# Fused attention and two feed-forward layers: low parts of the second layer's weights made by adding transfers, 16 weights converted early

## The chip, the cores and the metric

The kernel runs on one core of a Trainium2 chip. The metric is the device time of one launch in microseconds (us), the median of several runs; lower is better.

## What is computed

The reference chains three blocks, all in float32. The weights arrive as 64-bit floats.

```python
scores = scale * np.matmul(q, k.transpose(0, 1, 3, 2))        # 2 x 12 heads, 448 x 448, head 64
scores = np.einsum('bhij,hg->bgij', scores, w_pre)            # heads mixed before the softmax
attn = softmax(scores)
attn = np.einsum('bhij,hg->bgij', attn, w_post)               # and after it
x = np.matmul(attn, v)                                        # 896 tokens x 768
h = x @ w_in;  x = (h * sigmoid(1.702 * h)) @ w_out           # first layer, 768 -> 2048 -> 768
h = x @ w_in2; out = (P(h) / Q(h)) @ w_out2                   # second layer, cubic over quadratic
```

## The kernel before, in words

**Stages.** The attention takes some 240 us, the first layer follows to about 476 us, the second to the end. The attention works in chunks of 120 query rows and groups of 10 rows by 12 heads: scores (line 301), a transfer that regroups rows (330), a matmul that mixes heads (335), maximum, exponential, normalising, the second mix (368), and the product with v (387).

**The layers.** A layer has 32 *up* steps (16 column tiles `ft`, two halves of the tokens each, 18 matmuls of 448 columns) and 24 *down* weights (four groups `qq` of six, 24 matmuls for both halves). Each operand is kept as a high part, rounded to the matmul's format, and a low part, the rest; three matmuls (high by high, low weight by high, high by low) give one product (lines 613 to 615 and 680 to 682). So every weight tile needs, before TensorE may use it, a high part `w[:, 0]` and a low part `w[:, 1]`. `up` weights are 128x768, `down` weights 128x512; there are three buffers `wu` for the first and three `wd` for the second.

**Converting a weight.** `w_load` (564) brings the 64-bit words into a `raw` buffer on GpSimd's queue, two or three transfers for each weight. ScalarE takes the magnitude (`w_mag`, 569), VectorE makes the 32-bit float out of the words in four steps (`w_bits`, 574, 576, 578, 581) in a `wm` buffer. For the first layer the high part is then a cast (`w_part` with rest false, line 598 through 229 on ScalarE or 231 on VectorE) and the low part a subtraction on VectorE (595 through 234). The second layer's 40 weights (16 up, 24 down) are converted ahead, during the attention and the first layer, and stored as 32-bit floats in DRAM (`w_store`, 587, tiles d1u and d1d); in the second layer `w_fetch` (591) brings them back into a `raw` buffer, from which high and low parts are made in the same way. There are two raw buffers during the attention and three afterwards; a raw buffer is free again when the low part is made.

**The order of work.** A planner (`Plan.issue`) plays all steps through with estimated costs, each step having a rank, and writes each engine's instructions in the order in which its play issues them. It is a fixed order on each engine and queue: an instruction that waits holds back all behind it. Where the play finds TensorE busy for less than 55% of the last 2.6 us and nothing to do, it puts in pairs of matmuls on a tile of ones (`filler`, line 223), whose result nobody reads. `EARLY` is the number of second-layer weights whose ranks are spread over the attention; the others have ranks in the first layer, though a step can be issued before its rank's time where its engine has nothing else ready.

**The passage from attention to first layer.** The buffers of the attention are given up and those of the layers are set up when the last product with v is done (`open_late`, 512): a small transfer brings in `cab` (528), ScalarE takes absolute values of two of its columns (529), and everything behind that on ScalarE waits for it.

Of the kernel before, what the change touches and what calls it, by code (L numbers as in the profile page):

```python
# [12 lines left out]
AF = mybir.ActivationFunctionType  # L13
ALU = mybir.AluOpType
# [16 lines left out]
W_LAG = 4500  # L31

RANK = dict(k=-45, q=-45, v=-45, sc=-14, sco=-14, rg=-37, pre=-3, max=-3, exp=-6, n0=-9, n1=-9, n2=-4, post=1, phi=-4)
# [8 lines left out]
    whi=dict(act=0, dve=800),  # L42
    wlo=dict(dve=0),
# [12 lines left out]
NQ = NF // FQ  # L56
TB = 12
TAIL = 2
EARLY = 24
MID = 54  # L60
QC = 1.0 + 1e-6

# [128 lines left out]
def f(ap):  # L191
    return ap.bitcast(F32)
# [10 lines left out]
def talking_heads_then_two_ffn(ctx: ExitStack, tc: tile.TileContext, q, k, v, wpre, wpost, win1, wout1, win2, wout2, ab, out):  # L203
    nc = tc.nc
    pe, act, dve, pool, sp = nc.tensor, nc.scalar, nc.vector, nc.gpsimd, nc.sync
# [21 lines left out]
    def cast(eng, o, i):  # L227
        if eng is act:
            act.activation(o, i, AF.Copy)  # L229
        else:  # L230
            dve.tensor_copy(o, i)

    def sub(eng, o, a, b):
        eng.tensor_tensor(o, a, b, ALU.subtract)  # L234
# [30 lines left out]
    t_ = {}  # L265
# [157 lines left out]
    def step(name, ways, ns, deps, rank, fn, *args, **kw):  # L423
        if isinstance(ways, str):
            ways = [(ways, ns)]
        ways = [(*w, 0)[:3] for w in ways]
        plan.add(name, ways, deps, rank, lambda e: fn(*[engines[e] if x is None else x for x in args]), **kw)


    def copying(n, who, psum=False):  # L430
        cost = {"act": 94 - 42 * psum + 0.833 * n, "dve": 60 + (1.05 if psum else 0.54) * n}
        return [(e, cost[e], x) for e, x in PREF[who].items() if x is not None]

    def joining(n, who):
        cost = {"dve": 68 + 1.042 * n, "pool": 149 + 2.103 * n}
        return [(e, cost[e], x) for e, x in PREF[who].items() if x is not None]
# [3 lines left out]
    def mark(name, deps, give):  # L440
        plan.add(name, (), deps, 0, give=give)
# [11 lines left out]
    for ci, (b, c) in enumerate(chunks):  # L453
# [5 lines left out]
        for hp in range(NP):  # L459
            if ci == 0 and hp in (2, 3):  # L460
                for o in range(2):
                    n, e = (("sc1", 0, hp), ("sco1", 0, hp)) if o else (("sc", 0, hp), ("sco", 0, hp))
# [70 lines left out]
    def held(b, *n):  # L533
        k = plan.bank[n, b]
        if b == "wu" and not tiles[b]:
            wu = keep.tile([128, H * S], F32R, tag="wu", name="wu")
            tiles[b] = [wu[:, 2 * DM * i : 2 * DM * (i + 1)] for i in range(3)]
        if k >= len(tiles.get(b, ())):
            open_late()
        return tiles[b][k]  # L540
# [7 lines left out]
    def wcols(key):  # L548
        return DM if key[1] == "u" else FQ * 128
# [41 lines left out]
        pool.dma_start(t_["wf", key], t_["wd", key])  # L591

    def w_part(key, eng, rest):
        if rest:
            sub(eng, t_["w", key][:, 1], f(t_["wf", key]), f(t_["w", key][:, 0]))
        else:
            w = t_["w", key] = held("w" + key[1], "whi", key)[:, : 2 * wcols(key)].rearrange("p (s f) -> p s f", s=2)
            cast(eng, w[:, 0], f(t_["wf", key]))

    XN = {}  # L600

# [128 lines left out]
    for u in units:  # L730
        key = (u[1], "u", u[2]) if u[0] == "up" else (u[1], "d", u[2] * KK + u[3])
# [4 lines left out]
    def w_steps(key, c, rk):  # L736
        step(("wmag", key), "act", 90 + 760 * c, [d_raw[key]], rk + RANK["wmag"], w_mag, key, take=["wm"])
        for i in range(4):
            d0 = [("wb", key, i - 1)] if i else [("wmag", key)]
            kw = dict(give=[("raw", d_raw[key])]) if i == 3 else {}  # L740
            step(("wb", key, i), "dve", 60 + (400, 400, 810, 810)[i] * c, d0, rk, w_bits, key, i, **kw)
# [3 lines left out]
    for key, us in uses.items():  # L745

        p = NG - 30 + 8 * key[2] if key[:2] == (0, "u") and key[2] < 3 else rank[us[0]]
        c = wcols(key) / DM
        if key in ahead:
            j = ahead.index(key)  # L750
            e = (NG - 12) * (j + 0.5) / EARLY + RANK["ahead"]
            if j >= EARLY:
                e = NG + RANK["ffn"] + MID * (j - EARLY + 0.5) / (len(ahead) - EARLY)
            step(("eld", key), "pool", 3600 * c, [("hold",)], e + RANK["wld"], w_load, ("eld", key), key, take=["raw"], lag=W_LAG)
            w_steps(key, c, e + RANK["wb"])
            step(("est", key), "pool", 2000 * c, [("wb", key, 3)], e, w_store, key, give=[("wm", ("wmag", key))], lag=W_LAG)
            step(("wld", key), "pool", 2000 * c, [("est", key)], p + RANK["wld"], w_fetch, key, take=["raw"], lag=W_LAG)
            src = ("raw", ("wld", key))
        else:
            step(("wld", key), "pool", 3600 * c, [("hold",)], p + RANK["wld"], w_load, ("wld", key), key, take=["raw"], lag=W_LAG)  # L760
            w_steps(key, c, p + RANK["wb"])
            src = ("wm", ("wmag", key))
        d0 = [("wld", key) if key in ahead else ("wb", key, 3)]
        step(("whi", key), copying(wcols(key), "whi"), 0, d0, p + RANK["whi"], w_part, key, None, False, take=["w" + key[1]])
        step(("w", key), joining(wcols(key), "wlo"), 0, [("whi", key)], p + RANK["wlo"], w_part, key, None, True, give=[src])
        mark(("wend", key), us, [("w" + key[1], ("whi", key))])
    chunks_of = [[ci for ci, (b, c) in enumerate(chunks) if b == hf] for hf in range(2)]
    for L in range(2):
        for ft in range(NF):
            qq = ft // FQ  # L770
            for hf in range(2):
                key = (L, ft, hf)
                u = ("up",) + key
                p = rank[u]
# [37 lines left out]
        for qq in range(NQ):  # L812
            for u in downs(L, qq):
                _, _, _, m, halves = u
                p = rank[u]
# [88 lines left out]
```

## Time and profile before

| | before |
|---|---|
| time, median of 3 runs | 713.13 us (712.88 to 713.31) |
| span of the profiled execution, first to last instruction | 712.1 us |
| the profiled execution's own time | not listed; the runs' median is 1.0 us above its span |
| TensorE busy | 704.0 us (99%), 4230 matmuls |
| VectorE busy | 557.3 us (78%) |
| ScalarE busy | 406.7 us (57%) |
| GpSimd busy | 162.7 us (23%) |
| granted clock of TensorE | 0.999 |

The matmuls are pipelined: the busy time of one reaches into the next. What a matmul costs in a stream is the distance from its start to the next one's start; in the layers these distances are 0.2 us, where a single matmul's row says 0.37. So a busy share of 99% says that TensorE had something to do, and lost time must be looked for in the distances.

### The profile page before, as it was taken

How to read it: one execution, taken by the hardware profiler on the slowest of the kernel's cores; microseconds unless marked ns; L12 is line 12 of the kernel's file. 1: busy time of each engine (PE TensorE's matmuls, PEld its weight loads, DVE VectorE, ACT ScalarE, POOL GpSimd, SP SyncE). 2: the span in 40 equal slices, each digit the busy share in tenths (PEclk: the TensorE clock that was granted, in tenths of full speed). 3: DMA queues.
4: the chain of work that ended last, by engine and by line, in shares of the span. 5: the costliest groups of instructions: out<-in, count | busy, mean ns of one | idle time of the engine just before them, and what ended most of it. 6: DMA issues, size and time to landing. Idle time of an engine off the chain costs nothing.

```text
span 712.1 us, 11642 instructions
## 1 busy us (share of the span) xinstructions
PE 704.0 (99%) x4230; PEld 599.7 (84%) x4230; DVE 557.3 (78%) x1109; ACT 406.7 (57%) x764; POOL 162.7 (23%) x300
## 2 busy tenths in 40 slices
PE   8999999999999999999999999999999999999997
PEld 5666767767768889999999999999999999999997
DVE  2778678787888488887988898969999699789632
ACT  3678686786786445555452443348887565357310
POOL 0423222321323343343333323110001100100000
PEclk9999999999999999999999999999999999999999
DMA  5888877686563555555554544331112212111122
GB/s 190 247 264 278 285 234 250 221 280 220 177 222 129 175 172 185 183 187 176 178 177 163 161 143 168 112 100 52 53 38 60 81 38 74 53 30 29 31 82 104
DMA packets 40215, 106.85 MB, mean 150 GB/s; under 512 B 6622, under 2 KB 20446, under 8 KB 40158
## 3 DMA queue, kind: packets, MB, share of 16 engines
q0 software_dynamic: 23040, 76.89, 33.2%
q1 hardware_dynamic: 16830, 28.85, 11.9%
q8 instruction: 33, 0.54, 0.3%
q10 hardware_dynamic: 288, 0.37, 0.1%
q14 instruction: 24, 0.20, 0.1%
HBM read 71.49 MB, written 15.34 MB: 122 GB/s over the span
## 4 chain that ended last, share of the span: by engine, by line
PE 94%; DMA 3%; DVE 1%; ACT 1%; issue 1%; POOL 0%; ACTq 0%; DVEq 0%; SPq 0%
PE mm L680 11%; PE mm L682 11%; PE mm L681 11%; PE bk L613 11%; PE bk L614 11%; PE bk L615 10%; PE bk L368 10%; PE bk L335 9%; PE bk L387 5%; PE mm L301 5%; DMA d1u<-wmk 1%; DMA raw<-in_wout_dram 1%; PE bk L223 1%; DMA T<-S 0%; DMA cab<-in_ab_dram 0%
## 5 line engine op out<-in xcount | busy, mean ns | idle before, releaser
L680 PE MATMUL mm<-g,wd 128*128 128x448 f32 x384 | 141.7, 369 | 0.0
L682 PE MATMUL mm<-g,wd 128*128 128x448 f32 x384 | 140.3, 365 | 0.0
L681 PE MATMUL mm<-g,wd 128*128 128x448 f32 x384 | 140.2, 365 | 0.0
L368 PEld LDWEIGHTS bk<-W,E 120*112 120x112 f32 (+1 forms) x720 | 84.2, 177 | 33.6 <-issue 22.2
L368 PE MATMUL bk<-W,E 120*112 120x120 f32 (+1 forms) x720 | 88.2, 268 | 0.0
L335 PE MATMUL bk<-T,wpr 120*120 120x448 f32 (+1 forms) x180 | 81.8, 547 | 0.7 <-DMA T<-S 0.7
L680 PEld LDWEIGHTS mm<-g,wd 128*128 128x128 f32 x384 | 72.1, 188 | 5.8
L682 PEld LDWEIGHTS mm<-g,wd 128*128 128x128 f32 x384 | 72.1, 188 | 5.7
L681 PEld LDWEIGHTS mm<-g,wd 128*128 128x128 f32 x384 | 72.2, 188 | 5.4
L564 POOL DMA_DIRECT2D rawk<-in_win_dram x81 | 44.9, 561 | 136.5 <-issue 18.1
L341 DVE TENSOR_REDUCE sm<-bk 120x1 f32<-120x448 f32 (+1 forms) x90 | 55.7, 620 | 25.3 <-PE bk L335 24.3
L613 PE MATMUL bk<-xh,wu 128*128 128x448 f32 x192 | 70.7, 368 | 1.5 <-ACT t L623 1.5
L614 PE MATMUL bk<-xh,wu 128*128 128x448 f32 x192 | 70.3, 366 | 0.5 <-DVE wu L234 0.5
L613 PE MATMUL bk<-xn,wu 128*128 128x448 f32 x192 | 70.4, 367 | 0.0
L615 PE MATMUL bk<-xh,wu 128*128 128x448 f32 x192 | 70.2, 366 | 0.0
L614 PE MATMUL bk<-xn,wu 128*128 128x448 f32 x192 | 70.1, 365 | 0.0
L615 PE MATMUL bk<-xn,wu 128*128 128x448 f32 x192 | 70.1, 365 | 0.0
L237 DVE TENSOR_TENSOR yt<-mm,yt 128x896 f32<-128x896 f32 (+1 forms) x43 | 40.2, 936 | 36.9 <-PE mm L682 36.0
L229 ACT ACTIVATE AT<-bk 112x480 f32<-112x480 f32 (+1 forms) x87 | 50.4, 580 | 27.2 <-PE bk L368 26.5
L564 POOL DMA_DIRECT2D rawk<-in_wout_dram x70 | 38.7, 558 | 96.4 <-issue 26.1
L347 ACT ACTIVATE E<-bk,sm 120x448 f32<-120x448 f32 (+1 forms) x90 | 56.5, 628 | 3.5 <-DVE sm L341 1.6
L634 DVE SCALAR_TENSOR_TENSOR t<-t,cab,bk 128x448 f32<-128x448 f32 x64 | 43.4, 678 | 15.9 <-ACT t L630 10.9
(109 smaller groups left out, 1301.1 us busy)
## 6 DMA issues: line engine op xcount, KB each, us to landing
rawk<-in_win_dram POOLq DMA_DIRECT2D x81, 256.0 KB, 3.9
T<-S SPq DMA_DIRECT2D x86, 210.0 KB
rawk<-in_wout_dram POOLq DMA_DIRECT2D x70, 256.0 KB, 3.5
raw<-in_wout_dram POOLq DMA_DIRECT2D x26, 256.0 KB, 3.2
d1d<-wmk POOLq DMA_DIRECT2D x22, 256.0 KB, 4.4
d1u<-wmk POOLq DMA_DIRECT2D x28, 192.0 KB, 4.6
rawk<-d1u POOLq DMA_DIRECT2D x14, 384.0 KB, 3.3
raw<-in_win_dram POOLq DMA_DIRECT2D x15, 256.0 KB, 3.1
```

Of the source, the lines that this page charges most:

```text
L229: act.activation(o, i, AF.Copy)
L335: pe.matmul(p[:K, :S], wpr[:K, :K], t_["T", t][:K], start=True, stop=True)
L341: dve.tensor_reduce(t_["sm", t][:K, 0:1], t_["pre", t][:K, :S], AX.X, ALU.max, negate=True)
L347: act.activation(t_["E", t][:K], t_["pre", t][:K, :S], AF.Exp, bias=sm[:K, 0:1], scale=1.0, accum_out=sm[:K, 1:2])
L368: pe.matmul(o, t_["E", t][:K, jc * CP : jc * CP + CP], t_["W", t][:K], start=True, stop=True)
L564: pool.dma_start(r[:, c : c + 256], src[:, c : c + 256])
L613: pe.matmul(p[:, :S], w[:, 0, ws], x[:, 0, kk], start=kk == 0, stop=False)
L614: pe.matmul(p[:, :S], w[:, 1, ws], x[:, 0, kk], start=False, stop=False)
L615: pe.matmul(p[:, :S], w[:, 0, ws], x[:, 1, kk], start=False, stop=kk == KK - 1)
L680: pe.matmul(p[:, hf, :S], w[:, 0, ms], gt[:, 0, i, cs], start=i == 0, stop=False)
L681: pe.matmul(p[:, hf, :S], w[:, 1, ms], gt[:, 0, i, cs], start=False, stop=False)
L682: pe.matmul(p[:, hf, :S], w[:, 0, ms], gt[:, 1, i, cs], start=False, stop=i == FQ - 1)
```

## The change

Four things are changed. The low part of a second-layer weight is no longer a subtraction on VectorE: ScalarE writes the negative of the high part into the place of the low part (`w_minus`, a new step `wn`), and a transfer on GpSimd's queue adds the 32-bit weight from the raw buffer to it (`accum_op=ALU.add`). `EARLY` goes from 24 to 16. The planner's costs for the queue's steps are lowered (3600 to 2000, 2000 to 1200 and 2000 to 700 ns). With these the planner writes a new order on all engines.

```diff
-EARLY = 24
+EARLY = 16
...
     def w_part(key, eng, rest):
-        if rest:
+        if rest and eng is pool:
+            pool.dma_start(t_["w", key][:, 1], f(t_["wf", key]), accum_op=ALU.add)
+        elif rest:
             sub(eng, t_["w", key][:, 1], f(t_["wf", key]), f(t_["w", key][:, 0]))
...
+    def w_minus(key):
+        act.activation(t_["w", key][:, 1], f(t_["w", key][:, 0]), AF.Copy, scale=-1.0)
...
-            step(("eld", key), "pool", 3600 * c, [("hold",)], e + RANK["wld"], w_load, ("eld", key), key, take=["raw"], lag=W_LAG)
+            step(("eld", key), "pool", 2000 * c, [("hold",)], e + RANK["wld"], w_load, ("eld", key), key, take=["raw"], lag=W_LAG)
...
-            step(("est", key), "pool", 2000 * c, [("wb", key, 3)], e, w_store, key, give=[("wm", ("wmag", key))], lag=W_LAG)
-            step(("wld", key), "pool", 2000 * c, [("est", key)], p + RANK["wld"], w_fetch, key, take=["raw"], lag=W_LAG)
+            step(("est", key), "pool", 1200 * c, [("wb", key, 3)], e, w_store, key, give=[("wm", ("wmag", key))], lag=W_LAG)
+            step(("wld", key), "pool", 700 * c, [("est", key)], p + RANK["wld"], w_fetch, key, take=["raw"], lag=W_LAG)
...
-        step(("w", key), joining(wcols(key), "wlo"), 0, [("whi", key)], p + RANK["wlo"], w_part, key, None, True, give=[src])
+        if key[0] == 0:
+            step(("w", key), joining(wcols(key), "wlo"), 0, [("whi", key)], p + RANK["wlo"], w_part, key, None, True, give=[src])
+        else:
+            step(("wn", key), "act", 52 + 0.833 * wcols(key), [("whi", key)], p + RANK["wlo"], w_minus, key)
+            step(("w", key), "pool", 700, [("wn", key)], p + RANK["wlo"], w_part, key, None, True, give=[src], lag=5000)
```

Line numbers of the changed kernel are larger: by 5 from `up` on (618 stands for 613, 628 for 623), the adding transfer is line 595 and the negative copy line 603.

**ScalarE at the passage from the attention to the first layer.** `xh` is the last chunk's attention output, `t` the gate's result (line 623, then 628), `wu` a weight's high part. Before:

```order
L229 ACTIVATE xh_1700<-bk_67 128x3x88
L529 ACTIVATE cab<-cab 128x2
L623 ACT_TABLE_LOAD
L623 ACTIVATE t_2495<-bk_69 128x448
L229 ACTIVATE xh_1700<-bk_68 128x3x88
L229 ACTIVATE g_2493<-t_2495 128x448
L623 ACTIVATE t_2496<-bk_66 128x448
L569 ACTIVATE wmk_81<-rawk_79 128x768
```

and now:

```order
L229 ACTIVATE xh_1686<-bk_69 128x3x88
L529 ACTIVATE cab<-cab 128x2
L569 ACTIVATE wm_2453<-rawk_78 128x768
L229 ACTIVATE xh_1686<-bk_66 128x3x88
L628 ACT_TABLE_LOAD
L628 ACTIVATE t_2459<-bk_67 128x448
L229 ACTIVATE g_2457<-t_2459 128x448
L569 ACTIVATE wmk_80<-rawk_79 128x512
L229 ACTIVATE wu<-wmk_81 128x768
```

The first gate result frees bank 69 before and bank 67 now, and the second half of `xh` has moved ahead of it; the cast of the fourth weight, `wu<-wmk_81`, stands two rows behind that gate's high part.

**VectorE, the conversion of the fourth up weight** (the first `wu` that is not made during the attention). Before, the steps 574 to 581 on `wmk_80` and the low part stand among the first layer's work on `g`:

```order
L574 TENSOR_SCALAR wmk_80<-wmk_80 128x768
L576 TENSOR_SCALAR wmk_80<-wmk_80 128x768
L578 SCALAR_TENSOR_TENSOR wmk_80<-rawk_78,wmk_80 128x768
L234 TENSOR_TENSOR g_2493<-t_2496,g_2493 128x448
L581 SCALAR_TENSOR_TENSOR wmk_80<-rawk_78,wmk_80 128x768
L231 CAST g_2493<-t_2497 128x448
L234 TENSOR_TENSOR wu<-wmk_80,wu 128x768
```

and now its last two steps, on `wmk_81`, stand among the maxima of the attention's last groups:

```order
L341 TENSOR_REDUCE sm_2286<-bk_67 120x1
L578 SCALAR_TENSOR_TENSOR wmk_81<-rawk_78,wmk_81 128x768
L341 TENSOR_REDUCE sm_2296<-bk_69 120x1
L353 TENSOR_SCALAR sm_2286<-sm_2286 120x1
L581 SCALAR_TENSOR_TENSOR wmk_81<-rawk_78,wmk_81 128x768
L355 RECIPROCAL sm_2286<-sm_2286 120x1
```

The conversion moved from behind the fourth gate result into the attention.

**GpSimd's queue where the second layer's fetches begin.** Before, fetches alone:

```order
L587 DMA d1d_4148<-wmk_81 128x512
L591 DMA rawk_78<-d1u_517 128x768
L591 DMA rawk_79<-d1u_565 128x768
L591 DMA rawk_78<-d1u_682 128x768
L591 DMA raw_2488<-d1u_727 128x768
```

and now fetches and adding transfers (595) in turn:

```order
L591 DMA raw_2452<-d1u_514 128x768
L591 DMA rawk_78<-d1u_538 128x768
L595 DMA wu<-raw_2452 128x768
L591 DMA rawk_79<-d1u_669 128x768
L591 DMA raw_2452<-d1u_700 128x768
L595 DMA wu<-rawk_78 128x768
L595 DMA wu<-rawk_79 128x768
L591 DMA rawk_78<-d1u_853 128x768
L591 DMA rawk_79<-d1d_860 128x512
L595 DMA wd_2454<-rawk_79 128x512
L591 DMA rawk_79<-d1u_996 128x768
```

A fetch into a raw buffer now stands behind the adding transfer that reads that buffer, on the same queue.

## Rows read from the trace of the kernel before

**Rows 1.** The page: shares of the chain that ended last.
```profile
PE 94%; DMA 3%; DVE 1%; ACT 1%; issue 1%; POOL 0%; ACTq 0%; DVEq 0%; SPq 0%
```
**Rows 2.** Waits of TensorE: us in total, times, longest.
```profile
PE bk L613 <- ACT t L623: 1.5, 1, 1.5
```
**Rows 3.** TensorE in order of time: start us, us, instruction, idle before and releaser.
```profile
240.79 0.37 PE L615 MATMUL bk<-xh,wu 128*128 128x448 f32 x1
242.68 0.47 PE L613 MATMUL bk<-xh,wu 128*128 128x448 f32 x1 [1.51 <-ACT t L623]
242.98 0.36 PE L614 MATMUL bk<-xh,wu 128*128 128x448 f32 x1
243.18 0.36 PE L615 MATMUL bk<-xh,wu 128*128 128x448 f32 x1
...
257.37 1.73 PE L223 MATMUL bk<-warm 128*128 128x240 f32 x14
258.93 0.43 PE L613 MATMUL bk<-xh,wu 128*128 128x448 f32 x1
259.89 0.47 PE L614 MATMUL bk<-xh,wu 128*128 128x448 f32 x1 [0.52 <-DVE wu L234]
...
325.95 0.61 PE L223 MATMUL bk<-warm 128*128 128x240 f32 x4
326.40 0.36 PE L613 MATMUL bk<-xh,wu 128*128 128x448 f32 x1
```
**Rows 4.** ScalarE in order of time, at the passage and before the fourth weight's cast.
```profile
240.58 0.20 ACT L529 ACTIVATE cab<-cab 128x2 f32<-128x2 f32 x1 [3.43 <-DMA cab<-in_ab_dram]
240.79 1.28 ACT L623 ACT_TABLE_LOAD   x1
242.08 0.54 ACT L623 ACTIVATE t<-bk 128x448 f32<-128x448 f32 x1
242.52 0.39 ACT L229 ACTIVATE xh<-bk 128x264 fp32r<-128x264 f32 x1
...
258.01 0.84 ACT L229 ACTIVATE wu<-wmk 128x768 fp32r<-128x768 f32 x1
258.74 0.90 ACT L569 ACTIVATE wmk<-rawk 128x768 f32<-128x768 f32 x1
```
**Rows 5.** VectorE in order of time, the fourth up weight.
```profile
255.65 0.95 DVE L581 SCALAR_TENSOR_TENSOR wmk<-rawk,wmk 128x768 int32<-128x768 int32 x1
...
258.88 0.96 DVE L234 TENSOR_TENSOR wu<-wmk,wu 128x768 fp32r<-128x768 f32 x1 [0.34 <-ACT wu L229]
```
**Rows 6.** The chain that ended last, pieces in time: start us, us, what.
```profile
39.31 1.00 PE bk L368 x8
...
41.07 0.82 PE bk L368 x8
```
**Rows 7.** Groups of VectorE: low parts of fetched weights; busy us, mean ns.
```profile
L234 DVE TENSOR_TENSOR wu<-rawk,wu 128x768 fp32r<-128x768 f32 x14 | 13.4, 954 | 0.3
...
L234 DVE TENSOR_TENSOR wd<-rawk,wd 128x512 fp32r<-128x512 f32 x14 | 9.6, 683 | 0.0
```
**Rows 8.** Stretches: us, busy us of PE, PEld, DVE, ACT, POOL; clock, DMA share, GB/s.
```profile
245.00:455.00 210.00, 209.48 (x1044) 193.86 (x1043) 181.04 (x294) 95.66 (x152) 74.53 (x135) 1.00 0.51 170
476.00:703.00 227.00, 227.00 (x1125) 210.16 (x1124) 178.25 (x290) 130.03 (x221) 18.29 (x34) 1.00 0.18 55
481.00:534.00 53.00, 53.00 (x263) 48.83 (x262) 51.53 (x88) 43.53 (x79) 4.30 (x8) 1.00 0.16 48
```
**Rows 9.** Issues on GpSimd's queue: KB each, median us from issue to landing.
```profile
rawk<-d1u POOLq DMA_DIRECT2D x14, 384.0 KB, 3.3
...
rawk<-d1d POOLq DMA_DIRECT2D x14, 256.0 KB, 3.0
```
**Rows 10.** The last down weight: ScalarE's cast, and the unit that TensorE starts then.
```profile
693.31 0.19 PE L673 MATMUL mm<-warm 128*128 128x64 f32 x1
...
693.51 0.63 ACT L229 ACTIVATE wd<-rawk 128x512 fp32r<-128x512 f32 x1 [4.24 <-PE mm L682]
```

More of the change, by code (lines that the diff above doesn't have):

```diff
@@ L753, in talking_heads_then_two_ffn @@
                 e = NG + RANK["ffn"] + MID * (j - EARLY + 0.5) / (len(ahead) - EARLY)
-            step(("eld", key), "pool", 3600 * c, [("hold",)], e + RANK["wld"], w_load, ("eld", key), key, take=["raw"], lag=W_LAG)
+            step(("eld", key), "pool", 2000 * c, [("hold",)], e + RANK["wld"], w_load, ("eld", key), key, take=["raw"], lag=W_LAG)
             w_steps(key, c, e + RANK["wb"])
-            step(("est", key), "pool", 2000 * c, [("wb", key, 3)], e, w_store, key, give=[("wm", ("wmag", key))], lag=W_LAG)
-            step(("wld", key), "pool", 2000 * c, [("est", key)], p + RANK["wld"], w_fetch, key, take=["raw"], lag=W_LAG)
+            step(("est", key), "pool", 1200 * c, [("wb", key, 3)], e, w_store, key, give=[("wm", ("wmag", key))], lag=W_LAG)
+            step(("wld", key), "pool", 700 * c, [("est", key)], p + RANK["wld"], w_fetch, key, take=["raw"], lag=W_LAG)
             src = ("raw", ("wld", key))
         else:
-            step(("wld", key), "pool", 3600 * c, [("hold",)], p + RANK["wld"], w_load, ("wld", key), key, take=["raw"], lag=W_LAG)
+            step(("wld", key), "pool", 2000 * c, [("hold",)], p + RANK["wld"], w_load, ("wld", key), key, take=["raw"], lag=W_LAG)
             w_steps(key, c, p + RANK["wb"])
```

## The prediction

> **What bounds the kernel now.** I read first the chain that ended last: 94% of it is TensorE [rows 1]. So time can be won or lost only where TensorE does something needless or stands still. The list of its waits is short, and the longest is 1.5 us [rows 2]. Because a busy matmul row hides small gaps, I then read TensorE in order of time and took the distances from start to start. In a stream of 448-column matmuls it is 0.20 us (242.98 to 243.18), and an up step of 18 starts 3.65 us after the one before, a down unit of 24 some 4.87 us. After the start-up I find three places where the distance is larger or the work is idle, all in the first layer [rows 3]:
>
> - At 240.79 the next matmul starts 1.89 us later, 1.69 more than the stream.
> - At 257.37 stand 14 matmuls on the tile of ones, 1.56 us; then one real matmul, after which 0.96 us pass, 0.76 too many.
> - At 325.95 stand 4 more of them, 0.45 us.
>
> Together 4.46 us. Everything else, the whole second layer included, runs at the pace of the matmuls: TensorE is busy for 227.00 of 227 us there [rows 8]. That sets the size of what can be expected: the gain cannot be much over 4.5 us, whatever VectorE is relieved of, while a new wait can cost any amount.
>
> **What causes the three places.** The first is the passage out of the attention. ScalarE waits 3.43 us for the transfer of `cab`, then loads a table for 1.28 us, and only then makes the first gate result, which frees the bank that TensorE wants [rows 4]. The second is the fourth up weight: its last conversion step runs at 255.65, its high part at 258.01 behind a gate, its low part at 258.88 [rows 4, 5]; the planner saw this coming and put the 14 idle matmuls there. The third place is planned alike.
>
> **The change part by part.** *Subtractions removed.* 16 of 0.954 us and 24 of 0.683 us [rows 7] are 31.7 us of VectorE in the second layer. VectorE is busy for 178 of 227 us there, TensorE waits for it nowhere [rows 8]: worth nothing to the time.
>
> *Negative copies added.* 40 on ScalarE. No row shows this copy; the high part's cast has the same shape and engine, 0.84 us for an up weight [rows 4] and 0.63 for a down weight [rows 10], so about 28.6 us. ScalarE goes from 130 to some 159 of 227 us. The tight piece is 481 to 534, where it is busy for 43.5 of 53 us [rows 8]: some 9 weights pass there (40 x 53/227), 7 us more, about 50.5 of 53. VectorE, at 51.5 now, falls to about 44 in the same piece, and each gate passes through both engines, so I cost the exchange at nothing. Its cover is the rest of ScalarE's idle time there, 2.5 us; without it up to 3 us.
>
> *Adding transfers.* 40 more on GpSimd's queue, 0.54 us of issue each (18.29 us by 34 [rows 8]). What is unknown is L, the time from issue to landing; no row of before shows such a transfer. The nearest is the fetch of the same bytes on the same queue: 3.3 us for an up weight, 3.0 for a down weight [rows 9]. The Trainium skill speaks against taking that: "Collectives: The Full Stack", section "The bandwidth ceiling: the fold count and why AG ≠ RS ≠ AR", says that an add inside the DMA engines needs two source reads instead of one and so ran at half a copy's rate; no run here shows it yet, and by it 3.3 us would become at most 6.6, still inside the room worked out next. My own bounds are the fetch's 3.0 and twice 3.3, since the transfer has a sum to form and its destination to read; I take 5, the middle.
>
> The room: a down weight's buffer is free when its unit ends, and two more units run before the weight is wanted, 9.74 us. The chain is now 0.20 us hand-over (693.31 to 693.51), cast 0.63, 0.20, copy 0.63, 0.20, issue 0.54, then L [rows 10]: 2.4 + L, so L may be 7.3. For an up weight the two units are four up steps, 14.6 us, and the chain 2.8 + L: 11.8. The queue has its own limit. A fetch must wait until the transfer that reads its raw buffer has landed, and behind a waiting fetch stand the next weights' transfers. The new order has 25 turns from a transfer to a fetch; if each cost L, with 80 issues of 0.54, the queue needs 25 L + 43 us, and 227 us are there: L may be 7.35. At 5 both have room: 168 us of queue, and 2.3 us at the tightest weight. Raw buffers stay held some 6 us longer, but (11.6 us a cycle over three) gives one weight in 3.9 us where one in 5.7 is used. Cost: nothing.
>
> *The new order.* This is where I expect the gain. At the passage TensorE now has 60 matmuls (12.2 us) between the last product with v and the first bank that needs a gate result, against 12 (2.4 us) before. It would ask for that bank 9.8 us after 240.99, at 250.8, and the gate, now behind a magnitude (0.90) and the `xh` cast (0.39), ends at 242.62 + 1.29 = 243.9 [rows 4]. The 1.69 us go. The second half of `xh` is late next: cast by 242.1, VectorE about 0.4 after it, wanted after 30 matmuls, at 244.7. The fourth up weight's conversion has moved into the attention, and its cast stands two rows behind the first gate's high part, so it is ready by about 250 where before it was 259.8. The 0.76 us go, and there is no need for the 14 idle matmuls; the order holds neither these nor the 4: 1.56 and 0.45 us go.
>
> *What pays for it.* By the order, the attention converts 25 weights in place of 27 and the first layer 55 in place of 53. Two weights are at most eight steps of 0.96 us, 7.7, less three subtractions of 0.95 and one of 0.68 that leave this stage: VectorE gets about 4 us more where it has 29 idle (210 - 181 [rows 8]). Nothing. In the attention, the mix behind a scores block costs 1.00 us instead of 0.82 [rows 6], and the new order has 13 such places instead of 11: 0.4 us more.
>
> Sum: -1.69 - 1.56 - 0.76 - 0.45 + 0.4 = -4.1 us. The span becomes 708.0; the runs' median lies 1.0 us above the span of the profile, so **709.1 us**.
>
> **The rivals.** *A slow landing* (the other side). If L is over 7.3, every turn of the queue and every down weight at the end waits. At L = 7.6 the queue needs 233 us where 227 are there, 6 too many, and the last down weights come 0.3 us late, two or three times: 709.1 + 7 = 716. Each further 0.1 us of L adds up to 2.5. For it speaks only that the operation is unseen; against it that fetches land in 3.3, and that the queue does nothing else there.
>
> *The idle matmuls only stood in for a wait.* If the fourth weight is as late as now, or another takes its place, TensorE stands still in their stead. Gone is then at most the 1.69 of the passage, less the 0.4: about 711.8, perhaps 712.5. Against it speaks the place of the conversion in the new order.
>
> *ScalarE becomes late* between 481 and 534: up to 3 us come back, 709 to 712. For it speaks 95% load on an engine that works in a fixed order behind VectorE's results; against it that TensorE works through banks ahead of the gates, and that VectorE is faster there.
>
> **How the numbers follow.** The measurement can tell about 0.2% from no change, 1.4 us. The forecast, 708.2 to 710.5, gets 0.62, all faster. ScalarE late gets 0.14 (0.10 faster, 0.04 the same), idle matmuls that stood for a wait 0.12 (the same), the slow landing 0.12 (slower). Faster 0.72, the same 0.16, slower 0.12. The range goes from 708.2, where even the 0.4 of the attention fails to appear and other small gaps close, to 713.2, above the second and third rival; it leaves out the slow landing and a little at both ends.
>
> **What would show it.** Right: no distance over 0.3 us near the passage and at the fourth up weight, 28 of the filler matmuls of 240 columns instead of 46, no wait of TensorE for `wu` or `wd`, adding transfers landing in 3 to 6.6 us, VectorE's busy time lower by some 28 us. Wrong: TensorE waiting for a DMA into `wu` or `wd` in the second layer; fetches on GpSimd's queue that wait longer than 7 us for a transfer; a gap of TensorE in the first layer that ends with a weight's low part.

## The result, and the profile after

The changed kernel takes 722.85 us by the median (720.86 to 724.34), the kernel before 713.02 in the same session: a ratio of 1.0134, with an interval of 1.0116 to 1.0152. It is slower by 1.3%; 709.1 us was predicted, with a range up to 713.2. The profiled execution's span is 720.7 us against 712.1, 8.6 more.

What TensorE waits for now, in us in total, times, and the longest; no wait of this kind over 0.2 us stood there before:

```profile
PE bk L335 <- ACT AT L229: 7.2, 4, 3.8
PE bk L368 <- ACT AT L229: 2.1, 1, 2.1
```

Both belong to the attention: `AT` holds the attention weights that ScalarE copies out of a PSUM bank behind the second mix, and L335 and L368 want that bank. The stretches, first of the kernel before, then of the changed one (columns as in [rows 8]). The last three are taken 8.6 us later than in [rows 8], since the layers start that much later now, so that they hold the same pieces of work:

```profile
20.00:240.00 220.00, 219.76 (x1844) 158.66 (x1841) 169.71 (x477) 159.68 (x357) 64.18 (x117) 1.00 0.70 231
```

```profile
20.00:240.00 220.00, 210.55 (x1690) 147.62 (x1687) 161.03 (x452) 153.56 (x349) 56.79 (x104) 0.99 0.65 217
253.60:463.60 210.00, 210.00 (x1039) 194.15 (x1038) 189.73 (x316) 102.51 (x161) 83.18 (x150) 1.00 0.56 185
484.60:711.60 227.00, 227.00 (x1126) 210.41 (x1125) 152.79 (x249) 155.06 (x262) 50.55 (x69) 1.00 0.46 104
489.60:542.60 53.00, 53.00 (x264) 49.13 (x263) 48.61 (x85) 49.35 (x89) 12.54 (x17) 1.00 0.44 93
```

TensorE lost 9.2 us in the attention, where it had been busy throughout. The first layer has no idle stretch any more (210.00 against 209.48, and none of the 18 idle matmuls), and the second is as full as before, with VectorE lighter by 25 us and ScalarE heavier by 25. So TensorE went through the layers as predicted, and the loss lies ahead of them: the 8.6 us, and the 4.46 that the layers gained and the total does not show, 13.1 us.

**Where one stall comes from.** The largest stands between 90.58 and 95.33. The chain of waits there (start us, us, what):

```profile
84.21 0.21 POOL d1u L587
84.42 0.32 issue
84.74 9.07 DMA d1u<-wmk
...
93.92 0.07 ACT wmk L569
...
94.71 0.58 ACT AT L229
95.29 0.04 issue
95.33 1.05 PE bk L335 x2
```

A weight's store reads `wmk` for 9.07 us. ScalarE wants to write the next magnitude (L569) into that buffer, and behind it in ScalarE's fixed order stands the copy `AT`. ScalarE and then TensorE in order of time (start us, us, instruction, idle before and releaser):

```profile
89.43 0.20 ACT L347 ACTIVATION_READ_ACCUMULATOR E<-bk,sm 120x1 f32 x1
93.92 0.89 ACT L569 ACTIVATE wmk<-rawk 128x768 f32<-128x768 f32 x1 [4.28 <-DMA d1u<-wmk]
94.71 0.57 ACT L229 ACTIVATE AT<-bk 112x480 f32<-112x480 f32 x1
```

```profile
20.88 1.76 PE L335 MATMUL bk<-T,wpr 120*120 120x448 f32 x4
...
90.58 0.98 PE L368 MATMUL bk<-W,E 120*112 120x120 f32 x8
95.33 1.05 PE L335 MATMUL bk<-T,wpr 120*120 120x448 f32 x2 [3.77 <-ACT AT L229]
...
97.78 2.57 PE L335 MATMUL bk<-T,wpr 120*120 120x448 f32 x4
```

TensorE stands still for 3.77 us, and then four matmuls take 2.57 us that take 1.76 elsewhere. The stretches ahead of and behind this stall (the third number from the end is the granted clock, as a share of full speed):

```profile
84.00:90.00 6.00, 6.00 (x53) 4.67 (x50) 3.26 (x10) 2.85 (x7) 2.89 (x6) 1.00 1.02 318
...
95.30:100.30 5.00, 4.97 (x16) 3.04 (x16) 3.40 (x12) 3.47 (x10) 0.00 (x0) 0.66 0.28 99
```

At 0.66 instead of 1.00 for 5 us, the stall costs an estimated 1.7 us more (5 times 0.34).

The other four stalls of TensorE are of the same kind. ScalarE's magnitudes ahead of them, each with `AT` as the next instruction behind it:

```profile
56.91 0.89 ACT L569 ACTIVATE wmk<-rawk 128x768 f32<-128x768 f32 x1 [1.83 <-DMA d1u<-wmk]
...
61.69 0.89 ACT L569 ACTIVATE wmk<-rawk 128x768 f32<-128x768 f32 x1 [1.73 <-DMA d1u<-wmk]
...
124.77 0.90 ACT L569 ACTIVATE wmk<-rawk 128x768 f32<-128x768 f32 x1 [1.52 <-DMA d1u<-wmk]
...
130.49 0.89 ACT L569 ACTIVATE wmk<-rawk 128x768 f32<-128x768 f32 x1 [2.68 <-DMA d1d<-wmk]
```

Behind them TensorE waits 1.32, 1.43, 0.69 and 2.06 us; with the 3.77 these are all its waits for `AT`.

ScalarE's waits for such stores, over the whole run:

```profile
ACT wmk L569 <- DMA d1u<-wmk: 9.8, 5, 4.3
...
ACT wmk L569 <- DMA d1d<-wmk: 5.0, 3, 2.7
```

Before, they were 1.2 and 1.0 us. By the median the stores of the attention have not become slower: from issue to landing they took 5.1 us before (3.1 to 8.9) and take 4.8 now (3.2 to 9.6). At this place they are 1 to 2 us slower. What shrank more is the room. GpSimd's issues and ScalarE's magnitudes in the kernel before, at the like place:

```profile
80.09 1.08 POOL L587 DMA_DIRECT2D d1u<-wmk  x2
...
82.54 0.55 POOL L587 DMA_DIRECT2D d1d<-wmk  x1
```

```profile
87.96 0.92 ACT L569 ACTIVATE wmk<-rawk 128x768 f32<-128x768 f32 x1
91.11 0.67 ACT L569 ACTIVATE wmk<-rawk 128x512 f32<-128x512 f32 x1
```

There, 7.9 and 8.6 us lie between a store's issue and the magnitude, which finds its buffer free. In the changed kernel ScalarE comes to the magnitude at 89.6, 5.4 us after the issue at 84.20. The planner works out that room: it counts an up weight's store as done 1200 + 4500 ns after its issue now, 2000 + 4500 before. Here the store took 9.07 us.

### The profile page after: what moved, and what is told of

Same layout as the page of the kernel before. It is cut to its first block, busy times and chain, and to the rows that moved or that the text cites. A ratio compares the mean times of both kernels' runs of the same rounds, so it can differ in the third digit from the quotient of the medians.

```text
span 720.7 us, 11680 instructions
## 1 busy us (share of the span) xinstructions
PE 705.4 (98%) x4212; PEld 599.0 (83%) x4212; DVE 529.5 (73%) x1063; ACT 435.3 (60%) x810; POOL 198.8 (28%) x340
## 4 chain that ended last, share of the span: by engine, by line
PE 92%; DMA 5%; ACT 1%; issue 1%; DVE 0%; POOL 0%; SPq 0%; ACTq 0%
PE mm L685 11%; PE bk L618 11%; PE bk L620 11%; PE bk L619 11%; PE mm L687 11%; PE mm L686 11%; PE bk L368 9%; PE bk L335 8%; PE mm L301 5%; PE bk L387 4%; DMA d1u<-wmk 2%; DMA T<-S 2%; DMA d1d<-wmk 1%; PE bk L223 0%; ACT AT L229 0%
## 5 line engine op out<-in xcount | busy, mean ns | idle before, releaser
L368 PEld LDWEIGHTS bk<-W,E 120*112 120x112 f32 (+1 forms) x720 | 84.3, 178 | 37.1 <-issue 19.6
L368 PE MATMUL bk<-W,E 120*112 120x120 f32 (+1 forms) x720 | 89.6, 270 | 2.2 <-ACT AT L229 2.1
L335 PE MATMUL bk<-T,wpr 120*120 120x448 f32 (+1 forms) x180 | 82.6, 553 | 8.0 <-ACT AT L229 7.2
```

What stands on the lines that cost most here:

```text
L335: pe.matmul(p[:K, :S], wpr[:K, :K], t_["T", t][:K], start=True, stop=True)
L368: pe.matmul(o, t_["E", t][:K, jc * CP : jc * CP + CP], t_["W", t][:K], start=True, stop=True)
```

## The experiments

The theory was that the lowered costs alone do this. Two rivals: the spreading of 16 instead of 24 weights over the attention does it (`EARLY`); the adding transfers and their traffic do it. All ratios are to the kernel before, with their interval. Where a version's span is given, it is that of its one profiled execution.

| version | median us | ratio | interval |
|---|---|---|---|
| the change | 722.85 | 1.0134 | 1.0116 to 1.0152 |
| lowered costs alone | 726.19 | 1.0180 | 1.0164 to 1.0196 |
| the change with the old costs | 721.52 | 1.0106 | 1.0089 to 1.0123 |
| adding transfers alone | 713.75 | 0.9998 | 0.9988 to 1.0008 |
| the change, store counted done after 9000 ns | 714.16 | 1.0006 | 0.9995 to 1.0017 |
| the same after 7000 ns | 712.28 | 0.9989 | 0.9976 to 1.0002 |
| the change, stores send a constant tile | 717.96 | 1.0071 | 1.0057 to 1.0084 |
| 9000 ns, with subtractions | 715.39 | 1.0029 | 1.0018 to 1.0040 |
| 9000 ns and `cab` early | 708.77 | 0.9939 | 0.9927 to 0.9952 |
| 9000 ns, `cab` early, with subtractions | 708.79 | 0.9932 | 0.9920 to 0.9944 |
| before with `cab` early | 711.76 | 0.9982 | 0.9970 to 0.9994 |

**Lowered costs alone**, in the kernel before:

```diff
-            step(("eld", key), "pool", 3600 * c, ...
+            step(("eld", key), "pool", 2000 * c, ...
-            step(("est", key), "pool", 2000 * c, ...
+            step(("est", key), "pool", 1200 * c, ...
-            step(("wld", key), "pool", 2000 * c, [("est", key)], ...
+            step(("wld", key), "pool", 700 * c, [("est", key)], ...
-            step(("wld", key), "pool", 3600 * c, [("hold",)], ...
+            step(("wld", key), "pool", 2000 * c, [("hold",)], ...
```

> The kernel before with nothing but the four lowered costs; subtractions on VectorE and EARLY = 24 stay. Theory: ScalarE waits for stores that still read wmk, TensorE for AT by 5 us or more, 718 to 726 us. Both rivals: no more waits than in the kernel before, 712 to 714 us.

ScalarE's waits for stores in this run:

```profile
ACT wmk L569 <- DMA d1d<-wmk: 13.1, 10, 2.2
ACT wmk L569 <- DMA d1u<-wmk: 11.6, 7, 3.4
```

17 waits of 24.7 us together, and TensorE waits 9.0 us for `AT` in front of L335. The costs alone make such a loss, larger than the whole change does, as the theory had it; the time lies 0.2 us above its range.

**The change with the old costs** (the same four lines the other way round, in the changed kernel):

> The changed kernel with the planner's four old costs for loads, stores and fetches; the adding transfers and EARLY = 16 stay. Theory (the lowered costs let the planner put a magnitude on ScalarE before the store has read its buffer): TensorE's waits for AT fall from 9.3 us in all to under 2, the attention loses nothing, the gain at the passage stays; 709 to 712 us. Rival one (spreading 16 instead of 24 weights over the attention does it): the waits stay, 720 to 724. Rival two (the adding transfers and their traffic do it): 720 to 724 as well.

A miss: 721.5 us. The waits for stores are gone (0.7 us), but under the old costs this order has losses of its own. TensorE stands at a distance of 2.09 us at the passage, so the gain there is gone too. In the first layer it runs 40 idle matmuls (4.5 us) and stands at three distances of 1.1 to 1.2 us, because low parts of `wu` and `wd` come late. In the attention the chain shows this at the longest stop:

```profile
177.06 9.22 DMA T<-S
...
186.39 0.16 ACT S L229
...
187.21 0.57 ACT AT L229
...
187.82 1.01 PE bk L335 x2
```

The transfer that regroups rows reads `S` for 9.22 us, ScalarE's next copy into `S` waits for it, and `AT` stands behind that. It is the same kind of stall with another transfer. So the theory was too narrow: the costs are one way into it, not the only one. The time is that of the rivals (720 to 724), but not the mechanism that was named for the first, since the waits for stores did not stay. A version with `EARLY` = 16 and nothing else was not run, so that `EARLY` makes these losses without the adding transfers is argued, not shown. With `EARLY` = 24 the lowered costs add 1.8%, with 16 only some 0.3%, between intervals that overlap. Together the two parts partly make up for each other: the change has half as many waits for stores as the lowered costs alone (8 against 17 into `wmk`), and none of the idle matmuls and late weights in the first layer that this run has.

**Adding transfers alone**, in the kernel before, with the old costs and `EARLY` = 24:

> The kernel before with nothing but the negative copies and adding transfers; old costs, EARLY = 24. The order of the attention stays that of the kernel before. Theory: the adding transfers cost nothing and win nothing, or only what idle matmuls in the first layer gave up: 711 to 714 us, TensorE busy throughout the second layer. Rival two: the loss of the change shows here, 718 or more.

0.9998: nothing, in either direction. TensorE is as full in the second layer as in [rows 8], and the distances of [rows 3] are all there again. The second rival falls, for the order of the kernel before.

**The store counted done later**, one number in the changed kernel:

```diff
-            step(("est", key), ..., give=[("wm", ("wmag", key))], lag=W_LAG)
+            step(("est", key), ..., give=[("wm", ("wmag", key))], lag=9000)
```

> The changed kernel with one number altered: the planner counts a store as done 9000 ns after its issue ended instead of 4500, so it gives the wm buffer free later; all lowered costs stay. Theory: no magnitude is ordered before its buffer's store has landed (about 9 us in the attention), the waits of ScalarE for d1u and d1d fall from 14.8 to under 2 us, those of TensorE for AT from 9.3 to under 1: 708.5 to 711 us. If some other part of the change makes the loss: 718 or more.

The mechanism came out, the time did not: it lies 3 us above the range expected. No wait for `AT` is left in TensorE's list, and ScalarE's for stores are 0.8 us in all. The whole 1.3% is gone. But the time is that of the kernel before, because another loss has appeared at the passage. TensorE's wait, and the window behind it:

```profile
PE bk L618 <- ACT t L628: 3.3, 1, 3.3
```

```profile
244.00:248.00 4.00, 4.00 (x14) 3.56 (x13) 3.18 (x6) 1.39 (x3) 0.71 (x2) 0.57 0.02 6
```

In this order only 12 matmuls stand between the last product with `v` and the first bank that needs a gate, as in the kernel before, and ScalarE can use `cab` only from 241.03. The distance there is 3.71 us, and the granted clock is 0.57 for the next 4.

**The same with 7000 ns:**

> The changed kernel with the store counted done after 7000 ns in place of 4500 (9000 in the run that lost nothing). The played room from a store's issue to the magnitude that reuses its buffer is 7.8 to 12.7 us here, 5.3 to 9.2 in the change, 9.8 to 12.4 with 9000. Theory: ScalarE's waits for d1u and d1d fall from 14.8 us to under 4, TensorE's waits for AT under 4: 713 to 717 us, between the two. Rival (any new order has stalls of its own, whatever the room): 718 or more, and the waits that TensorE has don't go back to stores.

It does better than expected: 712.28 us. ScalarE's waits for stores are 2.1 us in three, and TensorE's list has 0.5 us for `AT`, with 1.4 at the passage. The rival falls here: two new orders with more room for the stores have both lost the stalls.

**Stores that send a constant tile**, which leaves the order as it is and takes the reason for the wait away. It leaves out the stored weights, so it serves for its time alone:

```diff
-    warm = keep.tile([128, 240], F32R, tag="warm", name="warm")
+    warm_ = keep.tile([128, 384], F32R, tag="warm", name="warm")
...
-            pool.dma_start(t_["wd", key][:, cs], t_["wf", key][:, cs])
+            if key[1] == "u":
+                pool.dma_start(t_["wd", key][:, cs], warm_.bitcast(I32))
+            else:
+                to = t_["wd", key].rearrange("p (a f) -> p a f", a=2)
+                pool.dma_start(to, bass.broadcast_tensor_aps(warm_[:, :256].bitcast(I32).rearrange("p (a f) -> p a f", a=1), to)[0])
```

> The changed kernel with its order untouched, but each store of a second-layer weight sends as many bytes from a constant tile of ones instead of the wm buffer (so the second layer works on weights of one). The stores still cross the same queue and load it as much; only nothing waits for them to read wm. Theory (the wait for the store to have read wm is the loss): ScalarE waits for no d1u or d1d, TensorE's 9.3 us of waits for AT fall under 1.5, and the time is what was predicted for the change, 708.5 to 711.5 us. If the transfers' mere load, or the new order itself, makes the loss: 718 to 724.

717.96 us: half of the loss is gone, 0.71% in the place of 1.34. That is 6.5 us above the theory's range and at the edge of the rival's (718 or more), so neither holds as it was put. No wait for a store is left, and TensorE's waits for `AT` fall from 9.3 to 5.0 us at two places. The chain at the second of them:

```profile
115.24 9.11 DMA rawk<-in_win_dram
124.38 0.03 ACT wmk L570
...
125.17 0.58 ACT AT L229
```

The magnitude now waits for the *load* of its weight, which took 9.11 us. In the planner's play it is counted done 2000 + 4500 ns after its issue. At the first place it is the same: the magnitude at 59.64 waited 2.77 us for a load. So the order itself still stalls, as the rival says, but in the way of the theory: the store was the last thing that ScalarE waited for, and the load on the same queue was close behind it. Without the waits for stores half of the loss is gone; the other half then stands behind loads.

**Subtractions in the place of adding transfers**, otherwise as with 9000 ns:

> Lowered costs, EARLY = 16 and the store counted done after 9000 ns, but low parts by subtractions on VectorE, as before the change. The attention's order is that of the run with 9000 ns. Theory: the adding transfers win and lose nothing where TensorE is the bound: the same as that run within 1 us, 713 to 715 us, TensorE busy throughout the second layer. Rival: VectorE is needed in the first layer's end, where subtractions come back: 716 or more.

715.39 us is 1.2 above its partner, more than the 1 us allowed and less than the rival's 716; by the ratios to the kernel before it is 0.23%, and the intervals just fail to meet. In the traces 0.3 us of it is at the passage (a distance of 4.01 us against 3.71), which both orders have; where the rest arises was not found. TensorE is as busy in the second layer as in its partner. The next pair, where the passage is mended, says it better.

**The constants of `cab` early**, on top of 9000 ns:

```diff
-        cab = lp.tile([128, 16], F32, tag="cab", name="cab")
-        sp.dma_start(cab[:, 0:6], ab)
+        cab = cab_
...
+    cab_ = keep.tile([128, 16], F32, tag="cab", name="cab")
+
     def hold_raw():
+        sp.dma_start(cab_[:, 0:6], ab)
```

> The run with the store counted done after 9000 ns, and besides it the six constants of cab brought in early in the attention instead of at the passage, so that ScalarE doesn't wait for their transfer there. Theory: the run before it lost 3.5 us of TensorE at the passage to that transfer (distance 3.71 us at 239.42) and some more in the matmuls that ran slower behind it; they come back: 3.5 to 5 us under that run, 709 to 711 us by the median, the span 706.5 to 708. If the gate waits for the attention's buffers anyway: no more than 1 us.

708.77 us, 0.9939: faster than both kernels, with a span of 706.9, and 5.4 us under the run with 9000 ns where at most 5 were expected (4.8 by the ratios). ScalarE at the passage:

```profile
237.01 0.20 ACT L528 ACTIVATE cab<-cab 128x2 f32<-128x2 f32 x1
238.57 1.28 ACT L630 ACT_TABLE_LOAD   x1 [1.37 <-PE bk L387]
239.87 0.55 ACT L630 ACTIVATE t<-bk 128x448 f32<-128x448 f32 x1
```

It waits 1.37 us for the last product with `v` and for no transfer; TensorE has no distance over 0.3 us left at the passage.

> The fastest version so far (EARLY = 16, lowered costs, the store counted done after 9000 ns, cab early; 0.9939 of the time before) with subtractions on VectorE in place of the adding transfers. Theory: with every stall of the attention gone TensorE is the bound throughout, and the adding transfers are worth nothing: 0.993 to 0.996. If VectorE's relief is what the first layer's end needs: 0.998 or more, with TensorE waiting for VectorE's low parts.

The same version with subtractions: 0.9932, the intervals overlap. Where neither a store nor the passage stalls, the adding transfers are worth nothing.

> The kernel before with the constants of cab brought in early, nothing else. Theory: the 1.69 us of the passage come back and no more: 0.9972 to 0.9985 of the time before. If the gate waits for the attention's buffers anyway: no difference.

0.9982, in the range expected: in the kernel before, the wait for `cab` was worth the 1.69 us of [rows 3] and not much more. The rest of what the two versions above won, 0.4 to 0.5%, comes with their order (`EARLY`, costs and the 9000 ns); no run takes these three apart.

## Why the prediction was wrong

**The step that failed** is the second half of "What pays for it": "In the attention, the mix behind a scores block costs 1.00 us instead of 0.82 [rows 6], and the new order has 13 such places instead of 11: 0.4 us more." The attention lost 13.1 us. At the stalls and in the slow matmuls behind them I find 11.3 to 12.5 of it, by whether each distance between two matmuls is taken against that between the same two kinds in the changed kernel or in the kernel before; the rest, 0.6 to 1.8, is spread over the new order and was not followed. In place of the 0.4 the runs showed waits of ScalarE for stores that still read `wmk` (14.8 us), which hold back `AT`, and TensorE with it for 9.3 us; with the store counted done after 9000 ns both are gone. I counted in that order how much work each engine gets and in which sequence on TensorE. What I did not do is set ScalarE's order against GpSimd's queue: where a magnitude writes into a buffer that a store still reads. The lowered costs were told in front of the prediction, but no term of the sum came from them. The run with the lowered costs alone shows that they make such a loss by themselves.

**The gains were right.** The 1.69 us of the passage, the 0.76 of the fourth up weight and the idle matmuls of 1.56 and 0.45 all went: none of these distances is in the changed kernel, and 28 filler matmuls are left, as forecast. The order with 9000 ns and `cab` early, which has neither the stalls nor the passage's wait, takes 708.77 us where 709.1 was forecast. It is another order than the one that the forecast was made for, so this supports the gain's size and does not prove the forecast.

**The second layer costs nothing: right**, and so was the room for L. The groups of issues on GpSimd's queue (KB each, median us from issue to landing):

```profile
rawk<-d1u POOLq DMA_DIRECT2D x11, 384.0 KB, 3.4
wu<-rawk POOLq DMA_DIRECT2D x11, 384.0 KB, 4.1
rawk<-d1d POOLq DMA_DIRECT2D x16, 256.0 KB, 3.2
wd<-rawk POOLq DMA_DIRECT2D x16, 256.0 KB, 3.4
...
raw<-d1u POOLq DMA_DIRECT2D x5, 384.0 KB, 5.1
wu<-raw POOLq DMA_DIRECT2D x5, 384.0 KB, 4.3
```

I took 5 between 3.0 and 6.6; it is 3.4 for a down weight and 4.1 to 4.3 for an up weight. The half rate that the Trainium skill ("Collectives: The Full Stack", section "The bandwidth ceiling: the fold count and why AG ≠ RS ≠ AR") measured for a collective of 16 MB that adds inside the DMA engines does not show at 256 and 384 KB: the adding transfer takes 0.84 to 1.21 times as long as the fetch of the same bytes into the same buffer (4.3 against 5.1, 4.1 against 3.4, 3.4 against 3.2). A plain copy from one on-chip buffer to another was not run, so the comparison is with a transfer from DRAM.

**ScalarE between 481 and 534.** In the same piece of the layer, 489.6 to 542.6 now, ScalarE is busy for 49.35 of 53 us, where I had 50.5, and VectorE for 48.61, where I had 44. ScalarE was loaded nearly as forecast, and VectorE was relieved by less than half of what I had. TensorE is busy throughout all the same, so that rival did not come about, nor did the slow landing of adding transfers.

**The rivals lacked the one that came.** The mishap on the slower side was looked for where the change adds an operation. It came where the change alters only the planner's numbers.

## What to carry to other kernels

Where a planner writes the order, its costs and lags are part of the program: a number that says when a buffer is free decides which engine stands in a fixed order behind which transfer. So each reuse of a buffer in the new order should be set against the longest landing that the trace shows, not the median. The same holds for loads, as the run with the constant tile shows. An engine's step that waits for a transfer should not stand ahead of one that frees a bank which TensorE wants; and before a new kind of work is judged, it should be run alone, with the planner's old numbers.

## What the runs showed of the hardware

A store of the same kind on the same queue lands after 3.1 to 8.9 us in the attention of the kernel before; the slow ones that I looked at fall where much else is under way. A stretch of the kernel before with full traffic (the last two columns are the DMA share and GB/s):

```profile
80.00:86.00 6.00, 6.00 (x42) 4.28 (x39) 4.20 (x12) 3.54 (x9) 2.79 (x6) 1.00 1.00 304
```

Here, and in the stretch from 84 to 90 us of the changed kernel shown above (1.02, 318 GB/s), the 16 DMA engines are busy throughout. The stores issued in them took 7.0 to 8.3 us before, 8.9 to 9.6 after. In the changed kernel GpSimd had issued three loads, three pieces of stores and two more loads in 4.3 us:

```profile
82.61 1.61 POOL L564 DMA_DIRECT2D rawk<-in_win_dram  x3 [10.33 <-ACT W L359]
84.20 1.08 POOL L587 DMA_DIRECT2D d1u<-wmk  x2
85.28 0.54 POOL L587 DMA_DIRECT2D d1d<-wmk  x1
85.81 1.08 POOL L564 DMA_DIRECT2D rawk<-in_wout_dram  x2
```

I had taken a landing from the second layer's quiet rows (3.0 to 3.3 us), where the DMA share is 0.18, and had none of the attention's. The Trainium skill ("DMA: Bandwidth & Descriptors", section "Anatomy of one DMA — SWDGE (gpsimd) path") fits the time of such a transfer by 2.0 us and the bytes over 436e3; that would be an estimated 2.5 us for a piece of 192 KB and 2.6 for one of 256. The quickest stores of the attention (3.1 and 3.2 us) come near it, the slowest (9.6 us) take nearly four times as long.

A stall of TensorE can cost more than its length: after 3.77 us without work the granted clock was 0.66 over 5 us, after 3.35 us at the passage of the 9000 ns run 0.57 over 4 us. With full speed at 2.4 GHz, both stretches ran for the most part at the lower level of 1.2. It need not: behind the 2.06 us stall of the changed kernel the clock stayed at 1.00 (131.9 to 137.0 us), and so it did behind one of 2.57 us in the run with the old costs (187.8 to 193.0), while behind one of 2.33 us in the run with the constant tile it was 0.66 over 5 us (61.0 to 66.0).
